# Softmax weights of a one-query attention laid out with four rows of one head side by side

## The chip, the core and the metric

The kernel runs on one core of a Trainium2 chip. The metric is device time in microseconds, the median of the runs of one kernel. Before the change it was 1253.28 us (three runs, 1253.01 to 1253.91). A profile shows the span of one execution on the device, some 2 us less than the time of the run.

## The reference

Eight batches of 32 heads, one query row per head, 4096 keys and values of 128 numbers each, all bfloat16:

```python
q: (8, 32, 1, 128)   k, v: (8, 32, 4096, 128)
scores = jnp.einsum('bhqd,bhkd->bhqk', q, k) * scale     # scale = 128 ** -0.5
attn = softmax(scores, axis=-1)
return jnp.einsum('bhqk,bhkd->bhqd', attn, v)
```

Every key and value is used once, for one multiply and one add, so there is little arithmetic per byte.

## The kernel before

The 256 heads are taken in 32 tiles of G = 8 heads. A tile of keys, kt, has 128 partitions, 16 for each head, and C = 256 rows per partition: 8 MB. VectorE (DVE) multiplies kt with the query and folds it in halves; TensorE (PE) adds up parts of it with an identity matrix; DVE reduces the result to scores, sc, 256 per partition. ScalarE (ACT) then makes the weights w. A value matmul here takes all 128 partitions of w and vt (128 x 32 and 128 x 512 in the profile of before) and sums over them, so w has a column for each of the eight heads at each row, and a bias of -1e30 makes those of foreign heads zero.

```python
sc_pool = ctx.enter_context(tc.tile_pool(name="sc_pool", bufs=1))
...
w = w_pool.tile([P, C, G], BF16, name="w", tag="w")
...
for g in range(G):
    nc.scalar.activation(
        out=w[:, :, g], in_=sc[:], func=ACT.Exp, bias=bias[:, g : g + 1], scale=scale,
        accum_out=esum[:, t % R, g : g + 1],
    )
```

A value matmul takes CB = 4 rows of w, 32 columns, as stationary operand and four rows of vt, 512 columns, as moving one. Its 32 x 512 result goes to one of four groups of PSUM partitions, av; the records of matmuls of different groups overlap (64 of them took 5.42 us in a middle tile, at a mean of 525 ns each). Only the blocks where the row of w equals the row of vt are wanted; a second matmul with a matrix of ones and zeros, pick, takes them out.

```python
group = [
    0 if t == NT - 1 and C // 2 <= c0 < C // 2 + 3 * C // 16 else c0 // CB % TG
    for c0 in range(0, end, CB)
]
for c0 in range(lo, hi, CB):
    i = c0 // CB
    j = group[i]
    nc.tensor.matmul(
        avs[t][j * AG : (j + 1) * AG, :], lhsT=w[:, c0 : c0 + CB, :],
        rhs=vt[:, c0 : c0 + CB, :], start=(i < TG), stop=(j not in group[i + 1 :]),
    )
...
for m in range(CB):      # result_of: pick the blocks out of the copy of av
    nc.tensor.matmul(
        ops[n][:], lhsT=pick[:, m, r, :], rhs=comb[:, m, :],
        start=(r == 0 and m == 0), stop=(r == R - 1 and m == CB - 1),
    )
```

In the last tile twelve successive matmuls go to one group, one after another. The last tile of vt comes in seven pieces of 128, 64, 32, 16, 8, 4 and 4 rows, so that its matmuls can follow the landings.

Of the kernel before, what the change touches and what calls it, by code (L numbers as in the profile page):

```python
# [7 lines left out]
ACT = mybir.ActivationFunctionType  # L8
ALU = mybir.AluOpType
AX = mybir.AxisListType  # L10
BF16 = mybir.dt.bfloat16
F32 = mybir.dt.float32

G = 8
KB, VB = 2, 1
TG = 4
R = 2
OB = 4
LAST = 4
# [4 lines left out]
def kernel(  # L24
# [7 lines left out]
    nc = tc.nc  # L32
    B, H, Sq, D = q.shape
    S = k.shape[2]
    P = nc.NUM_PARTITIONS
    assert Sq == 1 and D == 128
    NH = B * H
    PH = P // G
    C = S // PH
    NT = NH // G  # L40
    scale = float(D) ** -0.5
# [4 lines left out]
    CB = 4  # L46
    RG = R * G
    NQ = NT // R
    TB = 32
    AG = CB * G  # L50
    assert TG * AG == P and NH % P == 0 and P % G == 0 and TB % PH == 0 and C % CB == 0

    q_n = q.rearrange("b h o d -> (b h o) d").rearrange("(x p) d -> p x d", p=P)
    o_n = out.rearrange("b h o d -> (b h o) d").rearrange("(n u x) d -> n x u d", u=OB, x=RG)
# [7 lines left out]
    w_pool = ctx.enter_context(tc.tile_pool(name="w_pool", bufs=2))  # L62
# [14 lines left out]
        out=ident[:], in_=ident[:], pattern=[[-1, P]], compare_op=ALU.not_equal,  # L77
        fill=1.0, base=0, channel_multiplier=1,
# [5 lines left out]
        out=heads[:], in_=heads[:], pattern=[[-1, G], [0, PH]], compare_op=ALU.not_equal,  # L84
        fill=1.0, base=0, channel_multiplier=1,
# [5 lines left out]
        out=own[:], in_=own[:], pattern=[[-PH, G]], compare_op=ALU.is_ge,  # L91
        fill=NEG, base=0, channel_multiplier=1,
    )
    nc.gpsimd.affine_select(
        out=own[:], in_=own[:], pattern=[[PH, G]], compare_op=ALU.is_ge,
        fill=NEG, base=PH - 1, channel_multiplier=-1,
# [4 lines left out]
        out=same[:].rearrange("p (h x) -> p h x", x=PH),  # L101
        in_=own[:].rearrange("p (b h) -> p h b", h=TB // PH)
# [7 lines left out]
    for j in range(TG):  # L110
        part = pick[j * AG : (j + 1) * AG, :, :, :]
        nc.gpsimd.affine_select(
            out=part, in_=part, pattern=[[-G, CB], [G, R], [-1, RG]],
            compare_op=ALU.not_equal, fill=1.0, base=0, channel_multiplier=1,
        )
        nc.gpsimd.affine_select(
            out=part, in_=part, pattern=[[-G, CB], [0, R], [0, RG]],
            compare_op=ALU.is_ge, fill=0.0, base=0, channel_multiplier=1,
        )
        nc.gpsimd.affine_select(  # L120
            out=part, in_=part, pattern=[[G, CB], [0, R], [0, RG]],
            compare_op=ALU.is_ge, fill=0.0, base=G - 1, channel_multiplier=-1,
        )
    ones = consts.tile([P, 1], F32, name="ones")
    nc.vector.memset(ones[:], 1.0)
# [1 line left out]
    w_last = consts.tile([P, LAST, RG], BF16, name="w_last")  # L127
# [90 lines left out]
    def weights_of(t):  # L218
        sc = scs.pop(t)
        pmax = small.tile([P, 1], F32, name="pmax", tag="pmax")  # L220
        nc.vector.tensor_reduce(out=pmax[:], in_=sc[:], axis=AX.X, op=ALU.max)  # L221
        spread = small.tile([P, TB], F32, name="spread", tag="spread")
        nc.vector.tensor_scalar(  # L223
            out=spread[:], in0=same[:], scalar1=pmax[:, 0:1], scalar2=-scale,
            op0=ALU.add, op1=ALU.mult,
        )
        nmax = small.tile([P, 1], F32, name="nmax", tag="nmax")
        nc.vector.tensor_reduce(  # L228
            out=nmax[:], in_=spread[:], axis=AX.X, op=ALU.min, apply_transpose=True
        )  # L230
        bias = small.tile([P, G], F32, name="bias", tag="bias")
        nc.vector.tensor_scalar(  # L232
            out=bias[:], in0=own[:], scalar1=nmax[:, 0:1], scalar2=None, op0=ALU.add
        )
        w = w_pool.tile([P, C, G], BF16, name="w", tag="w")
        if t % R == 0:
            esums[t // R] = small.tile([P, R, G], F32, name="esum", tag="esum")
        esum = esums[t // R]
        for g in range(G):
            nc.scalar.activation(  # L240
                out=w[:, :, g], in_=sc[:], func=ACT.Exp, bias=bias[:, g : g + 1], scale=scale,
                accum_out=esum[:, t % R, g : g + 1],
            )
        ws[t] = w
        if t == NT - 1:
            nc.gpsimd.tensor_copy(out=w_last[:, :, RG - G : RG], in_=w[:, C - LAST : C, :])

    avs = {}

    def values_of(t, lo, hi):  # L250
        vt = loads["v", t]
        w = ws[t]
        if lo == 0:
            avs[t] = ps_v.tile([P, CB * D], F32, name="av", tag="av")
        end = C if t < NT - 1 else C - LAST
# [7 lines that stand above are left out]
            i = c0 // CB  # L263
            j = group[i]
            nc.tensor.matmul(  # L265
                avs[t][j * AG : (j + 1) * AG, :], lhsT=w[:, c0 : c0 + CB, :],
                rhs=vt[:, c0 : c0 + CB, :], start=(i < TG), stop=(j not in group[i + 1 :]),
            )

# [56 lines left out]
    with tc.manual_schedule():  # L326
        q_prep(0)
        for t in range(NT):
# [15 lines left out]
            if t > 0 and not v_last:  # L344
                values_of(t - 1, 0, C)
                copy_of(t - 1)
# [6 lines left out]
            if t > 0 and v_last:  # L353
                values_of(t - 1, 0, C)
            scores_of(t, 3)
            weights_of(t)
            if t > 0:
                if v_last:
                    copy_of(t - 1)
                if t % R == 0:  # L360
                    norm_of(n)
                result_of(t - 1)
        values_of(NT - 1, 0, C // 2)
        norm_of(NQ - 1)
        recip_of(NQ - 1)
# [34 lines left out]
```

## Time and profile before

| | before |
|---|---|
| time, us | 1253.28 |
| read from DRAM | 536.94 MB, at 429 GB/s over the span |
| busy share: DMA queue of k and v / DVE / PE / ACT | 99.4% / 83% / 40% / 27% |
| one exponential (ACTIVATE), ns | 1591 |
| read of its accumulator, ns | 496 |

The page of a profile gives busy shares in 40 slices, the chain of work that ended last, and groups of instructions with busy time and mean duration. The prediction shows these lines. One more group line belongs to them, that of the read of the sum that each exponential keeps (columns: line, engine, operation, names, shapes, count, then busy us, mean ns, idle time before):

```profile
L240 ACT ACTIVATION_READ_ACCUMULATOR w<-sc,bias 128x1 f32 x256 | 127.0, 496 | 0.0
```

There is one such read for each of the 256 exponentials, and its 496 ns overlap with the exponential that follows. Exponentials overlap too, so that 1591 ns is the time of one from start to end and not the time from one to the next. In the last group of the kernel before the starts lie some 1.1 us apart (start, duration, what):

```profile
1236.25 1.60 ACT L240 ACTIVATE w<-sc,bias 128x256 bf16<-128x256 f32 x1
1237.39 1.60 ACT L240 ACTIVATE w<-sc,bias 128x256 bf16<-128x256 f32 x1
```

### The profile page before, as it was taken

Reading aid. Unit: us, or ns where it says so; the run is one execution under the profiler, and the core shown is the slowest. Engines: PE = TensorE matmul, PEld = TensorE weight load, DVE = VectorE, ACT = ScalarE, POOL = GpSimd, SP = SyncE. Lnnn points to the kernel's source line nnn. Section 1 sums busy time; section 2 is a strip of 40 time slices with the busy share of each in tenths; the row PEclk is TensorE's granted clock in tenths of the full one; section 3 lists DMA queues with packets and bytes.
Section 4 is the critical chain, followed back from the end, with each engine's and each line's share of the span. In section 5 each row is a group of like instructions: output and inputs, shape, how many; then the busy total and the mean of one; then the engine's idle time right before and its main releaser. Section 6 shows DMA issues by size and latency. Waiting matters only on the chain.

```text
span 1251.5 us, 7723 instructions
## 1 busy us (share of the span) xinstructions
PE 501.8 (40%) x3067; PEld 176.1 (14%) x3067; DVE 1038.0 (83%) x588; ACT 343.8 (27%) x625; POOL 6.0 (0%) x26
## 2 busy tenths in 40 slices
PE   1334442444333443334533244432444334444455
PEld 0111110111111111111111111111111111111122
DVE  5888898888988889788898888987879888899981
ACT  0321233321333312333123331233321333213333
POOL 1000000000000000000000000000000000000000
PEclk9766655666556666566665666656666566666777
DMA  9999999999999999999999999999999999999997
GB/s 404 436 434 432 436 434 434 434 436 428 426 435 434 436 426 436 429 434 436 434 430 434 432 434 432 428 434 434 436 434 434 434 434 436 434 419 428 428 444 325
DMA packets 11444, 537.50 MB, mean 429 GB/s; under 512 B 1808, under 2 KB 2064, under 8 KB 2320
## 3 DMA queue, kind: packets, MB, share of 16 engines
q1 hardware_dynamic: 11072, 536.94, 99.4%
q8 instruction: 24, 0.39, 0.1%
q10 hardware_dynamic: 336, 0.07, 0.0%
q14 instruction: 12, 0.10, 0.0%
HBM read 536.94 MB, written 0.07 MB: 429 GB/s over the span
## 4 chain that ended last, share of the span: by engine, by line
DMA 76%; PE 15%; DVE 8%; issue 1%; SPq 0%; ACT 0%
DMA vt<-in_v_dram 75%; PE av L265 13%; DVE kt L179 5%; DVE kt L182 2%; PE ps L199 1%; DMA q_all<-in_q_dram 1%; DVE kt L187 0%; DVE sc L211 0%; SPq L146 0%; DVE pmax L221 0%; DVE spread L223 0%; DVE nmax L228 0%; ACT comb L292 0%; PE op L307 0%; ACT stage L316 0%
## 5 line engine op out<-in xcount | busy, mean ns | idle before, releaser
L179 DVE TENSOR_TENSOR kt<-kt,qb 128x8192 bf16<-128x8192 bf16 x128 | 565.1, 4415 | 91.3 <-DMA kt<-in_k_dram 79.8
L199 PE MATMUL ps<-kt,ident 128*128 128x512 bf16 x792 | 293.1, 529 | 662.8 <-DVE kt L187 507.4
L240 ACT ACTIVATE w<-sc,bias 128x256 bf16<-128x256 f32 x256 | 301.1, 1591 | 360.9 <-DVE bias L232 360.9
L182 DVE TENSOR_TENSOR kt<-kt 128x4096 bf16<-128x4096 bf16 x128 | 293.3, 2292 | 4.4
L199 PEld LDWEIGHTS <-ident 128*128 128x128 bf16 x792 | 92.0, 119 | 824.7 <-issue 670.0
L265 PE MATMUL av<-vt,w 128*32 128x512 bf16 x2047 | 181.0, 525 | 43.7 <-DMA vt<-in_v_dram 43.7
L211 DVE TENSOR_REDUCE sc<-ps 128x64 f32<-128x512 f32 x128 | 87.7, 685 | 87.0 <-PE ps L199 87.0
L292 ACT ACTIVATE comb<-av 128x512 bf16<-128x512 f32 x32 | 19.7, 616 | 413.2 <-PE av L265 413.2
L240 ACT ACTIVATION_READ_ACCUMULATOR w<-sc,bias 128x1 f32 x256 | 127.0, 496 | 0.0
L265 PEld LDWEIGHTS <-w 128*32 128x32 bf16 x2047 | 68.1, 127 | 167.7 <-issue 80.9
L187 DVE TENSOR_TENSOR kt<-kt 128x2048 bf16<-128x2048 bf16 x58 | 71.0, 1225 | 2.0
L162 ACT ACTIVATE qg<-qh 8x128 bf16<-8x128 f32 x32 | 8.5, 266 | 95.3 <-PE qh L158 95.3
L307 PE MATMUL op<-comb,pick 128*16 128x128 bf16 x128 | 16.4, 271 | 14.6 <-ACT comb L292 14.6
L221 DVE TENSOR_REDUCE pmax<-sc 128x1 f32<-128x256 f32 x32 | 13.4, 420 | 1.1
L285 DVE RECIPROCAL rz<-zp 16x1 f32<-16x1 f32 x16 | 2.4, 149 | 14.0 <-PE zp L277 14.0
L158 PE MATMUL qh<-q_all,ident 128*8 128x128 bf16 x32 | 8.5, 266 | 13.2 <-DMA q_all<-in_q_dram 13.2
L164 PE MATMUL qp<-qg,heads 8*128 8x128 bf16 x32 | 8.3, 258 | 12.7 <-ACT qg L162 12.7
L307 PEld LDWEIGHTS <-pick 128*16 128x16 bf16 x128 | 9.2, 104 | 26.2 <-issue 26.1
L316 ACT ACTIVATE stage<-op,rz 16x128 bf16<-16x128 f32 x16 | 6.2, 385 | 24.2 <-DVE rz L285 17.8
L166 ACT ACTIVATE qb<-qp 128x128 bf16<-128x128 f32 x32 | 8.9, 277 | 11.1 <-PE qp L164 11.1
L223 DVE TENSOR_SCALAR spread<-same,pmax 128x32 f32<-128x32 f32 x32 | 7.7, 241 | 1.1
L232 DVE TENSOR_SCALAR bias<-own,nmax 128x8 f32<-128x8 f32 x32 | 7.4, 231 | 1.1
(27 smaller groups left out, 26.8 us busy)
## 6 DMA issues: line engine op xcount, KB each, us to landing
kt<-in_k_dram SPq DMA_DIRECT2D x7, 4096.0 KB, 34.4
kt<-in_k_dram SPq DMA_DIRECT2D x2, 2048.0 KB, 36.7
vt<-in_v_dram SPq DMA_DIRECT2D x1, 4096.0 KB, 39.5
vt<-in_v_dram SPq DMA_DIRECT2D x1, 2048.0 KB, 44.0
vt<-in_v_dram SPq DMA_DIRECT2D x1, 1024.0 KB, 46.0
vt<-in_v_dram SPq DMA_DIRECT2D x1, 512.0 KB, 46.8
vt<-in_v_dram SPq DMA_DIRECT2D x31, 33.1
kt<-in_k_dram SPq DMA_DIRECT2D x28, 43.5
```

The lines of the kernel that those rows point to most:

```text
L158: nc.tensor.matmul(qh[:], lhsT=ident[:, p0 : p0 + G], rhs=q_all[:, x, :], start=True, stop=True)
L166: nc.scalar.activation(out=qb[:, 0, :], in_=qp[:], func=ACT.Copy)
L179: nc.vector.tensor_tensor(out=part, in0=part, in1=qb[:].to_broadcast([P, MC, D]), op=ALU.mult)
L182: nc.vector.tensor_tensor(out=part[:, :, 0 : D // 2], in0=part[:, :, 0 : D // 2], in1=part[:, :, D // 2 : D], op=ALU.add,)
L187: nc.vector.tensor_tensor(out=part[:, :, 0 : D // 4], in0=part[:, :, 0 : D // 4], in1=part[:, :, D // 4 : D // 2], op=ALU.add,)
L199: nc.tensor.matmul(ps[:], lhsT=ident[:], rhs=kt[:, u * UC : (u + 1) * UC, s * DS : (s + 1) * DS], start=(s == 0), stop=(s == n - 1),)
L211: nc.vector.tensor_reduce(out=scs[t][:, u * UC : (u + 1) * UC], in_=sums.pop((t, u))[:], axis=AX.X, op=ALU.add)
L221: nc.vector.tensor_reduce(out=pmax[:], in_=sc[:], axis=AX.X, op=ALU.max)
L240: nc.scalar.activation(out=w[:, :, g], in_=sc[:], func=ACT.Exp, bias=bias[:, g : g + 1], scale=scale, accum_out=esum[:, t % R, g : g + 1],)
L265: nc.tensor.matmul(avs[t][j * AG : (j + 1) * AG, :], lhsT=w[:, c0 : c0 + CB, :], rhs=vt[:, c0 : c0 + CB, :], start=(i < TG), stop=(j not i ...
L292: nc.scalar.activation(out=comb[:], in_=av, func=ACT.Copy)
L307: nc.tensor.matmul(ops[n][:], lhsT=pick[:, m, r, :], rhs=comb[:, m, :], start=(r == 0 and m == 0), stop=(r == R - 1 and m == CB - 1),)
```

## The change

One exponential writes a single head's weights. Before, these lie 16 bytes apart, with the seven other heads between them. The change puts four successive rows of one head side by side, 8 bytes, and steps 64 bytes from one such run to the next. The 32 columns of a value matmul are still 32 neighbouring numbers, now ordered by head and then by row, so pick gets another pattern (and needs two selects per group fewer) and the copy into w_last another order.

```diff
         nc.gpsimd.affine_select(
-            out=part, in_=part, pattern=[[-G, CB], [G, R], [-1, RG]],
+            out=part, in_=part, pattern=[[-1, CB], [CB * G, R], [-CB, RG]],
             compare_op=ALU.not_equal, fill=1.0, base=0, channel_multiplier=1,
         )
-        (two more affine_selects, which cleared what lay outside a row's heads)
...
-        w = w_pool.tile([P, C, G], BF16, name="w", tag="w")
+        w = w_pool.tile([P, C // CB, G, CB], BF16, name="w", tag="w")
...
+        sc_g = sc[:].rearrange("p (i m) -> p i m", m=CB)
         for g in range(G):
             nc.scalar.activation(
-                out=w[:, :, g], in_=sc[:], func=ACT.Exp, bias=bias[:, g : g + 1], scale=scale,
+                out=w[:, :, g, :], in_=sc_g, func=ACT.Exp, bias=bias[:, g : g + 1], scale=scale,
...
-            nc.gpsimd.tensor_copy(out=w_last[:, :, RG - G : RG], in_=w[:, C - LAST : C, :])
+            nc.gpsimd.tensor_copy(
+                out=w_last[:, :, RG - G : RG].rearrange("p m g -> p g m"),
+                in_=w[:, (C - LAST) // CB, :, :],
+            )
...
-                avs[t][j * AG : (j + 1) * AG, :], lhsT=w[:, c0 : c0 + CB, :],
+                avs[t][j * AG : (j + 1) * AG, :], lhsT=w[:, i, :, :],
```

More of the change, by code (lines that the diff above doesn't have):

```diff
@@ L50 @@
     AG = CB * G
-    assert TG * AG == P and NH % P == 0 and P % G == 0 and TB % PH == 0 and C % CB == 0
+    assert LAST == CB and TG * AG == P and NH % P == 0 and P % G == 0 and TB % PH == 0 and C % CB == 0
     q_n = q.rearrange("b h o d -> (b h o) d").rearrange("(x p) d -> p x d", p=P)
@@ L112 @@
         nc.gpsimd.affine_select(
-            out=part, in_=part, pattern=[[-G, CB], [G, R], [-1, RG]],
+            out=part, in_=part, pattern=[[-1, CB], [CB * G, R], [-CB, RG]],
             compare_op=ALU.not_equal, fill=1.0, base=0, channel_multiplier=1,
-        )
-        nc.gpsimd.affine_select(
-            out=part, in_=part, pattern=[[-G, CB], [0, R], [0, RG]],
-            compare_op=ALU.is_ge, fill=0.0, base=0, channel_multiplier=1,
-        )
-        nc.gpsimd.affine_select(
-            out=part, in_=part, pattern=[[G, CB], [0, R], [0, RG]],
-            compare_op=ALU.is_ge, fill=0.0, base=G - 1, channel_multiplier=-1,
         )
```

## The prediction

> **What bounds the kernel now.** I read the page's slices first, since they say whether any one resource is full from beginning to end.
>
> ```profile
> PE   1334442444333443334533244432444334444455
> ...
> DVE  5888898888988889788898888987879888899981
> ACT  0321233321333312333123331233321333213333
> ...
> DMA  9999999999999999999999999999999999999997
> GB/s 404 436 434 432 436 434 434 434 436 428 426 435 434 436 426 436 429 434 436 434 430 434 432 434 432 428 434 434 436 434 434 434 434 436 434 419 428 428 444 325
> ```
>
> Each digit is a tenth of busy time in one of 40 slices of 31.3 us. The row to look at is DMA: nine tenths or more in every slice but the last, and the rate row stands at 426 to 436 GB/s nearly throughout. DVE is high but not full, ACT mostly at two or three tenths. The DMA section of the page says how much has to come in.
>
> ```profile
> q1 hardware_dynamic: 11072, 536.94, 99.4%
> ...
> HBM read 536.94 MB, written 0.07 MB: 429 GB/s over the span
> ```
>
> Keys and values are read once, 536.94 MB. At the best common slice rate, 436 GB/s, that alone is 536.94 / 0.436 = 1231.5 us of the 1251.5 us span. So no change that leaves the bytes alone can take off more than 20.0 us (1.6%), and that bound also includes start and drain.
>
> Next the costly groups, for the lines that the change touches.
>
> ```profile
> L240 ACT ACTIVATE w<-sc,bias 128x256 bf16<-128x256 f32 x256 | 301.1, 1591 | 360.9 <-DVE bias L232 360.9
> L265 PE MATMUL av<-vt,w 128*32 128x512 bf16 x2047 | 181.0, 525 | 43.7 <-DMA vt<-in_v_dram 43.7
> L265 PEld LDWEIGHTS <-w 128*32 128x32 bf16 x2047 | 68.1, 127 | 167.7 <-issue 80.9
> ```
>
> After the bar stand busy us and mean ns of one, then the idle time before and what ended it. The exponentials take 1591 ns for 256 elements per partition; they wait for the maximum (bias), and the matmuls that use their result wait for vt from DRAM. No group shows PE waiting for the exponentials: w is ready before vt. The timeline of a middle tile agrees: the eight exponentials run from 623.5 to 632.9 us and the value matmuls that use them start at 645.65, when their vt lands. The slack is 12.8 us.
>
> Last the chain of waits at the end of the kernel, the one place where slack can vanish.
>
> ```profile
> 1200.13 46.92 DMA vt<-in_v_dram
> 1247.06 0.04 issue
> 1247.10 0.74 PE av L265 x3
> 1247.84 0.02 issue
> 1247.86 0.60 ACT comb L292
> 1248.47 0.04 issue
> 1248.51 0.40 PE op L307 x4
> 1248.91 0.02 issue
> 1248.93 0.36 ACT stage L316
> ```
>
> Columns are start, duration and what. The last pieces of vt land at 1247.06; three matmuls, a copy, four pick matmuls and a scaled copy follow, then the output's own DMA. The exponentials are not in it, but only just, as the timeline of PE shows:
>
> ```profile
> 1239.85 3.56 PE L265 MATMUL av<-vt,w 128*32 128x512 bf16 x29
> 1243.25 0.19 PE L277 MATMUL zp<-ones,esum 128*16 128x1 f32 x2
> 1243.30 3.61 PE L265 MATMUL av<-vt,w 128*32 128x512 bf16 x28
> 1247.10 0.72 PE L265 MATMUL av<-vt,w 128*32 128x512 bf16 x3 [0.19 <-DMA vt<-in_v_dram]
> ```
>
> The last tile's matmuls could not start before its exponentials ended (about 1239). They catch up at 1246.91 and still wait 0.19 us for the last vt. Two limits nearly meet there; DMA is the later one.
>
> [...]the copy of 512 elements takes 616 ns and that of 128 elements 277 ns (qb, line 166), so (616 - 277) / 384 = 0.88 ns per element, though both read PSUM.
> [...]in the two ten-microsecond windows filled with exponentials (623 to 633 and 662 to 672) DMA moved 439 and 446 GB/s; in the windows just after them 426 and 420. Slow writes do not cost DMA anything that could come back.
> [...]
>
> **The change part by part.**
> Exponentials. The count stays 256, the read of sc stays contiguous. [...] Issue spacing matters more for the group of eight: in the tail the starts are 1229.56, 1230.53, 1231.70 ... 1237.39, about 1.12 us apart, and the group ends near 1239.0, 9.4 us. [...] None of this is on the chain in the 31 tiles with slack of 12.8 us or so.
>
> Value matmuls. Still 2047 of them, with stationary columns that are 32 consecutive bf16 before and after; only their order differs. Loads stay at 127 ns, matmuls at 525 ns: 0. The pick matmuls likewise: 128 of 271 ns, another pattern of ones: 0.
>
> Prologue. Eight of twelve selects on POOL go, 8 x 0.34 = 2.7 us of POOL's 6.0 us. They end at about 7.1 us; pick is first used at 84.3 us. On the path: 0. The copy into w_last writes in another order, still 32 elements per partition; it took 0.21 us at 1239.1 and its user ran at 1247.77. Even at 1 us it stays hidden: 0.
>
> Tail. [...]the first half of vt lands near 1198.2 + 39.5 = 1237.7, taking the median to landing of the 4096 KB piece. So the first 32 matmuls start 1.8 us earlier, and then follow the pieces; the 0.19 us wait becomes longer, but the last landing, 1247.06, does not move. Its three matmuls and all that follow stay. Gain 0. A small loss is possible: PE now works in bursts, and its granted clock was 0.50 from 1239 to 1243 and 1.00 from 1244 on; should it be 0.50 at the end, three plus four plus four short matmuls, 0.72 + 0.38 + 0.38 us, might grow by 0.2 to 0.5 us.
>
> Sum: 1253.28 + 0 to 0.4, minus at most a few tenths for jitter in the order of DMA. I say 1253.3 us.
>
> **Rivals.**
> *Buffers come free earlier.* A faster ACT could free something that starts a load sooner. For: ACT also does the copy of av and q. Against: the copy in a middle tile (613.05) comes right after the matmuls, which ended by vt, and the issue of the next vt (612.99) preceded it; that queue already had the k tile in flight until 626.3, 13 us of supply. If wrong somewhere, the slices of 419 to 430 GB/s could rise to 434: some eight slices by 1 to 2%, 3 to 4 us, so 1249 to 1250.
> *The tail is bound by ACT rather than DMA.* For: only 0.19 us separates the two, and the DMA share drops to 0.54 to 0.68 from 1243 to 1247, so pieces may be there before the profile says. If all but the final four rows had landed early, the backlog of matmuls would vanish and the end could come up to 1 us sooner: 1252.3.
> *The new form is slower.* Each write of four is 8 bytes in a 64-byte step, and the output pattern has one dimension more. If it hurt, an exponential of 2500 ns would make the group 16 us: middle tiles still hide it under 12.8 us of slack plus nine already counted, but the tail would end 6 to 7 us later, about 1260. [...]
>
> **Range and chances.** Runs before spread over 0.9 us. The first rival gives the low side, the clock at the end and a different chip the high side: 1250.0 to 1255.5 us. Faster by over 2% needs 1228.2 us, below the 1231.5 us of pure transfer: 0.01. Slower by over 2% needs 1278.3, an exponential group some 34 us long: 0.01. Within 2%: 0.98.
>
> **What would show the steps right or wrong.** [...]the read of the accumulator, 496 ns, should stay. Loads and matmuls of av keep 127 and 525 ns within a few per cent; POOL has 18 instructions. DMA stays at 99% and 429 GB/s, the chain's end is again vt landing some 4.5 us before the span's end, with a longer wait ahead of the last av matmuls. A time below 1250 would say that ACT was releasing loads after all; one above 1256 that the new write or the clock of PE reached the tail.

The sum came to 1253.28 + 0 to 0.4 us, and the forecast to 1253.3 us. That the first 32 matmuls wait for the landing near 1237.7, and no longer for the exponentials, the profile after bears out (exponentials done at 1231.7, matmuls from 1237.35 on).

## The result

The kernel after took 1253.59 us (median of four runs, 1253.39 to 1253.93), the kernel before 1253.14 us in the same comparison. The ratio is 1.0003 with a 95% interval from 0.9985 to 1.002: the same. A ratio here is the mean time of one kernel's fast runs over that of the other's of the same rounds, so not quite the ratio of the medians.

The slices of the profile after, for ACT and DMA:

```profile
ACT  0111011111011110111101111011110111101111
...
DMA  9999999999999999999999999999999999999997
GB/s 404 436 434 434 436 434 436 432 436 432 434 437 430 431 432 432 436 432 434 432 432 432 436 436 434 434 425 430 433 430 434 432 432 436 432 430 431 427 448 308
```

ACT's digits fell from two or three to one; the DMA row did not change at all. Then the groups of the same kernel that answer to those of before:

```profile
L261 PE MATMUL av<-vt,w 128*32 128x512 bf16 x2047 | 183.5, 529 | 52.0 <-DMA vt<-in_v_dram 52.0
L233 ACT ACTIVATE w<-sc,bias 128x256 bf16<-128x256 f32 x256 | 126.3, 494 | 357.8 <-DVE bias L224 357.8
L261 PEld LDWEIGHTS <-w 128*32 128x32 bf16 x2047 | 67.8, 127 | 178.9 <-issue 86.8
L233 ACT ACTIVATION_READ_ACCUMULATOR w<-sc,bias 128x1 f32 x256 | 47.7, 186 | 0.0
```

An exponential fell from 1591 to 494 ns, and the read of its accumulator from 496 to 186 ns. From one start to the next it is now 0.49 us instead of some 1.1 us, so a group of eight takes 3.9 us instead of 9.4 us:

```profile
1228.23 0.49 ACT L233 ACTIVATE w<-sc,bias 128x256 bf16<-128x256 f32 x1
1228.72 0.49 ACT L233 ACTIVATE w<-sc,bias 128x256 bf16<-128x256 f32 x1
```

ACT's busy time was halved, from 343.8 to 172.6 us. The matmuls and loads of PE kept their durations. So 171 us of work went, and the time did not move. The end of the chain of waits of the kernel after (start, duration, what) differs from that of before:

```profile
1197.03 45.19 DMA vt<-in_v_dram
1242.22 0.04 issue
1242.26 6.08 PE av L261 x26
1248.34 0.02 issue
1248.36 0.61 ACT comb L288
```

Before, the chain came from the last landing of vt, at 1247.06, and the copy of av (comb) started at 1247.86. Here it comes from an earlier piece, landed at 1242.22, and 6.08 us of PE work; the copy starts 0.5 us later than before, although the loads were done no later (the DMA share is 0.00 from 1247 on). The experiments look into that, too.

### The profile page after: what moved, and what is told of

It is laid out like the page before. It is cut to its first block, busy times and chain, and to the rows that moved or that the text cites. A ratio compares the mean times of both kernels' runs of the same rounds, so it can differ in the third digit from the quotient of the medians.

```text
span 1252.0 us, 7714 instructions
## 1 busy us (share of the span) xinstructions
PE 503.5 (40%) x3067; PEld 175.8 (14%) x3067; DVE 1038.0 (83%) x588; ACT 172.6 (14%) x625; POOL 3.3 (0%) x18
## 4 chain that ended last, share of the span: by engine, by line
DMA 75%; PE 15%; DVE 8%; issue 1%; ACT 0%; SPq 0%
DMA vt<-in_v_dram 74%; PE av L261 14%; DVE kt L171 5%; DVE kt L174 2%; PE ps L191 1%; DMA q_all<-in_q_dram 1%; DVE kt L179 0%; DVE sc L203 0%; DVE pmax L213 0%; SPq L138 0%; DVE spread L215 0%; DVE nmax L220 0%; ACT comb L288 0%; PE op L303 0%; ACT stage L312 0%
## 5 line engine op out<-in xcount | busy, mean ns | idle before, releaser
L233 ACT ACTIVATE w<-sc,bias 128x256 bf16<-128x256 f32 x256 | 126.3, 494 | 357.8 <-DVE bias L224 357.8
L233 ACT ACTIVATION_READ_ACCUMULATOR w<-sc,bias 128x1 f32 x256 | 47.7, 186 | 0.0
L156 PE MATMUL qp<-qg,heads 8*128 8x128 bf16 x32 | 8.3, 259 | 12.7 <-ACT qg L154 12.7
```

Source lines behind the costliest of these rows:

```text
L233: nc.scalar.activation(out=w[:, :, g, :], in_=sc_g, func=ACT.Exp, bias=bias[:, g : g + 1], scale=scale, accum_out=esum[:, t % R, g : g + 1],)
```

## The experiments

All kernels passed the check of the result, except the two that load V only once, which are wrong. Twelve were run.

### What made an exponential slow

My theory was that a write is dear when none of the writes around it in time goes to a place near by. Three kernels change the order or place of the writes (and, to match, of what reads them) and nothing else. Each was run and profiled once. The first puts two rows side by side: 4 bytes, then a step of 32.

```diff
-        w = w_pool.tile([P, C // CB, G, CB], BF16, name="w", tag="w")
+        w = w_pool.tile([P, C // 2, G, 2], BF16, name="w", tag="w")
+        (sc_g, w_last, lhsT and pick to match)
```

> The kernel after with two rows of one head side by side instead of four: an exponential writes runs of 4 bytes with a step of 32 bytes[...]. Theory[...]: 494 ns as in the kernel after, ACT busy about 173 us. Rival (each jump costs something, and 64 jumps just hid under the other work): halfway, 650 to 1050 ns. Time unchanged by either, 1253 to 1254 us.

The second lets two heads alternate: four values of a head lie 4 bytes apart, so that no two of them are neighbours, and the next four begin 64 bytes on from these.

```diff
-        w = w_pool.tile([P, C // CB, G, CB], BF16, name="w", tag="w")
+        w = w_pool.tile([P, C // CB, G // 2, CB, 2], BF16, name="w", tag="w")
...
-                out=w[:, :, g, :], in_=sc_g, ...
+                out=w[:, :, g // 2, :, g % 2], in_=sc_g, ...
+        (w_last, lhsT and pick to match)
```

> The kernel after with the rows of two heads interleaved: an exponential writes single values 4 bytes apart[...], then jumps 32 or 64 bytes; no two of its writes are contiguous[...]. Theory[...]: 494 ns. Rival (contiguous runs count, each lone 2-byte write is dear): near 1600 ns as before, as there are 256 lone writes again. Time unchanged by either, 1253 to 1254 us.

The third fills the very places that the kernel after fills, but goes through all of them four times and each time writes one value of each run of four, 64 bytes from the one before.

```diff
-        sc_g = sc[:].rearrange("p (i m) -> p i m", m=CB)
+        sc_g = sc[:].rearrange("p (m i) -> p m i", m=CB)
...
-                out=w[:, :, g, :], in_=sc_g, ...
+                out=w[:, :, g, :].rearrange("p i m -> p m i"), in_=sc_g, ...
```

> The kernel after with the same places of w written by each exponential, but in another order: one value of each four, 64 bytes apart, then the second of each four, and so on; the scores are read in order as ever, so the weights are permuted and the result is wrong on purpose. [...] Time unchanged by either.

The two durations expected are near 1600 ns if it counts that successive writes are near each other, near 494 ns if only the places written count.

The result of this one was to be wrong, but the check passed it. The inputs q and k are normal numbers times 0.05, so the scaled scores spread by some 0.0025 (an estimate, 0.05 x 0.05) and all weights of a head are nearly equal. The check therefore doesn't tell a right order of weights from a wrong one; that the kernel after has them in the right places rests on reading its code.

The group of the exponentials in the profiles of the three, in this order, one fence for each; in the third, the read of the accumulator as well:

```profile
L235 ACT ACTIVATE w<-sc,bias 128x256 bf16<-128x256 f32 x256 | 127.4, 513 | 361.9 <-DVE bias L226 361.9
```

```profile
L235 ACT ACTIVATE w<-sc,bias 128x256 bf16<-128x256 f32 x256 | 134.0, 563 | 365.1 <-DVE bias L226 365.1
```

```profile
L233 ACT ACTIVATE w<-sc,bias 128x256 bf16<-128x256 f32 x256 | 298.3, 1582 | 356.1 <-DVE bias L224 356.1
L233 ACT ACTIVATION_READ_ACCUMULATOR w<-sc,bias 128x1 f32 x256 | 127.9, 500 | 0.0
```

Two values side by side suffice, but for 19 ns (513 against 494). Lone values 4 bytes apart cost 69 ns more than neighbours (563 against 494), no more, so runs without a gap are not what matters; where the 69 ns come from stays open. The third kernel fills the same places as the kernel after and takes 1582 ns, about as long as before, so not the places matter but the order. Writes whose neighbour in time lies 2 or 4 bytes away were fast (494, 513 and 563 ns), those 16 or 64 bytes from the next slow (1591 and 1582 ns); 8 bytes were not tried, and how nearness comes to count is not shown. The bytes written are the same in all three. The times, one run each, were 1253.05, 1253.98 and 1254.12 us, beside 1252.99 us of the kernel before for the first two and a median of 1253.22 us for the third: an exponential of 1582 ns or of 494 ns makes no difference to speak of.

### How much room there was

If loads bound the kernel, more exponentials should be free up to some limit. Both kernels were run with each group of eight done twice.

```diff
-        for g in range(G):
+        for g in list(range(G)) * 2:
             nc.scalar.activation(
```

> The kernel before with each group of eight exponentials run twice (same result). Theory (loads bound the kernel, the exponentials are hidden in every tile but the last, and in the last they just about meet the last landing): the group grows from 9.4 to some 18.8 us, still shorter than the 22 us between the first exponential of a middle tile (623.5) and the matmuls that use it (645.65), so middle tiles cost nothing; in the last tile the exponentials end 9.4 us later, 1248.4 instead of 1239.0, and the 12.5 us that follow them before the end follow again: about 1262 us, 9 us more. Rival A (hidden in the tail too, with room): within 1 us of 1253.3. Rival B (ACT releases loads in every tile): 32 times some microseconds, 1350 us or more.

> The kernel after with each group of eight exponentials run twice (same result). The group grows from 3.9 to 7.8 us; in the last tile it ends at 1235.5 instead of 1231.6, still ahead of the landing of the first half of the last vt at 1237.35. Theory: within 1 us of the kernel after (1253.6). Rival B (ACT releases loads): a good deal longer, 1270 us or more. Together with the other run this tells what the room is that the change made: 9.4 more us of exponentials cost 9 us before, 3.9 more cost nothing after.

The kernel after so doubled took 1254.6 us, ratio to before 1.0013 (0.9998 to 1.0028), as expected: 1.0 us from the 1253.59 us of the kernel after. But all four of its runs lie above all seven of the kernel before in the same rounds, by 1.6 us at the medians (1254.60 and 1252.99), and in its profile the last wait for vt ends at 1248.39, not at 1247.10 as in the kernel before; why is not shown. The kernel before so doubled took 1287.52 us, ratio 1.0272 (1.0257 to 1.0288), not 1262. Neither the theory nor a rival had that number. What DVE waited for in that run (total us, times, longest us):

```profile
DVE sc L211 <- PE ps L199: 103.4, 33, 9.9
DVE sc L211 <- ACT w L240: 87.8, 30, 5.3
```

The second line is new, and it stands in place of the 79.8 us for which DVE waits for loads of kt in the kernel before. The first reduction of the next tile's scores writes into sc, of which there is one buffer, and must wait until the last exponential has read the old scores. I had measured the room up to the reader of w: 12.8 us. The line that I had not looked at is in the timeline of DVE of the kernel before:

```profile
642.19 0.68 DVE L211 TENSOR_REDUCE sc<-ps 128x64 f32<-128x512 f32 x1
```

The exponentials ended at 632.9, so the room up to there was 9.3 us, and the doubled group needs 9.4 more. To test that, sc got two buffers. It takes 1 KB more per partition, and the store of results was made smaller along with it; a run with OB = 2 alone was not made.

```diff
-OB = 4
+OB = 2
...
-    sc_pool = ctx.enter_context(tc.tile_pool(name="sc_pool", bufs=1))
+    sc_pool = ctx.enter_context(tc.tile_pool(name="sc_pool", bufs=2))
+    (and the exponentials twice, as above)
```

> The kernel before with the exponentials run twice, and with two buffers for the scores (sc) instead of one; to make room the output stage holds 2 groups instead of 4, which makes the output's small stores more frequent. The run with doubled exponentials alone took 1287.5 us, not the 1262 expected; in its chain DVE's first sum of the next tile waits for the exponentials, which hold the only sc. Theory (that buffer is the nearest limit of a middle tile, 642.2 - 632.9 = 9.3 us of room in the kernel before, and not w with 12.8 us): with two buffers the wait of DVE for ACT goes, middle tiles are bound by loads again, and only the last two tiles pay, 9.4 us for the copy of av that PE waits for behind the exponentials of the last but one and 9.4 us for the last: about 1272 us. Rival (the order of ACT's own queue, where the query of the next tile stands behind the exponentials, is what holds the tiles up): 1284 us or more.

It took 1274.08 us, ratio 1.0164 (1.0147 to 1.0181), near the 1272 expected. In its list of waits DVE no longer waits for ACT because of sc. The rival's queue can be seen, PE waits 181.1 us in 32 times for the query behind the exponentials (12.7 us in the kernel before), but the time stays well under its 1284. What is left of the excess lies mostly in the last two tiles, in PE's timeline of this run:

```profile
1217.64 0.59 PE L307 MATMUL op<-comb,pick 128*16 128x128 bf16 x4 [16.78 <-ACT comb L292]
...
1261.00 0.37 PE L307 MATMUL op<-comb,pick 128*16 128x128 bf16 x2 [16.26 <-ACT comb L292]
```

PE stands idle for 16.78 and 16.26 us because the copy of av is queued on ACT behind a group of exponentials. In the kernel before the same two waits are 7.27 and 7.01 us, so they grew by 9.5 and 9.3 us. The 1262 expected of the first doubled run counted only one of the two. Ahead of the product DVE's waits are put down to ACT ten times in this run, 29.9 us, and to loads of kt 16 times, 52.9 us. Together that is 82.8 us in 26 waits, where the kernel before has 79.8 us in 25 for loads of kt; so the ten are probably waits for loads too, named wrongly by the profile. The last 2 us of the excess stay open.

### What the change is worth when loads are out of the way

V was loaded for the first tile only and used for all. The results are wrong.

```diff
     def load(kind, t):
+        if kind == "v" and t > 0:
+            loads["v", t] = loads["v", 0]
+            return
```

> The kernel before with V loaded for the first tile only and used for all (wrong result on purpose); half of the bytes go. Theory: loads need some 620 us then, and DVE's 1038 us of work become the bound: start 14.5 us, 1038 us, tail of exponentials 9.4 us, matmuls of the last tile 7.5 us and 5 us of drain, 1070 to 1090 us, with DVE over 94% busy. Rival B (ACT is on the path of every tile once loads are out of the way): DVE well under 94% busy and a time above 1120 us.

> The kernel after with V loaded for the first tile only (wrong result on purpose). Theory: DVE is the bound in every tile, ACT stays hidden, and the change is worth only what it takes off the last tile, where no load covers the exponentials: 9.4 - 3.9 = 5.5 us less than the kernel before with the same cut, so about 0.5% faster. Rival B: if ACT were on the path in each tile, up to 5.5 us a tile, 170 us less. Rival C (hidden in the tail too): no difference.

Before took 1178.43 us so, after 1171.72 us. Ratios to the unaltered kernel before are 0.9404 and 0.9347; one over the other gives 1.0061, 0.6% for the change, against the 0.5% expected. In the profiles both kernels had finished the last bias at the same time (1154.1 and 1154.3 us), and the last copy of results starts at 1172.60 and 1167.52: the whole difference comes after the last bias, in the one tile where no other work covers the exponentials. The lines are the last copy of results in before and in after, and then what DVE waited for in before:

```profile
1172.60 0.36 ACT L319 ACTIVATE stage<-op,rz 16x128 bf16<-16x128 f32 x1 [0.47 <-PE op L310]
1167.52 0.36 ACT L315 ACTIVATE stage<-op,rz 16x128 bf16<-16x128 f32 x1 [0.47 <-PE op L306]
...
DVE sc L214 <- PE ps L202: 94.1, 33, 3.1
```

The absolute times were some 90 to 110 us longer than I expected, and DVE was 88% busy and not 94%. By the signs that I had set (well under 94%, above 1120 us) that would be rival B for the kernel before. It is refuted all the same: the change gained 6.7 us and not 170, exponentials are 1.6% of the chain of before, and DVE's list of waits does not name them. My theory had left out a wait that the trace of before shows too: DVE stands idle some 3 us a tile until PE has added up the last part of the scores, 94 us in total here (87 in the kernel before).

### The end of the last tile

Four kernels were run together over five rounds: the kernel after once more; both kernels without the twelve matmuls in one group; and the kernel after without these and with matmuls that nobody reads, so that PE is not idle while pieces of vt land.

> The kernel after, unaltered, once more beside the kernel before and the variants of this call, over five rounds. Both theories: ratio within 0.2% of 1; in the profile the last value matmuls end about 1 us after the last load has landed, where before they ended 0.5 us after it.

```diff
-            0 if t == NT - 1 and C // 2 <= c0 < C // 2 + 3 * C // 16 else c0 // CB % TG
+            c0 // CB % TG
```

> The kernel after without the special grouping in the last tile that sends twelve successive value matmuls to one column group. Theory (in the kernel after, the twelve matmuls start cold, at a granted clock of 0.50 and some 0.43 us each[...]; 5.1 us in a row put the end of the value matmuls behind the last landing): without it [...]those of a piece end before the next piece lands, and the value matmuls end some 0.5 to 0.9 us sooner, right after the last landing, with a last wait on DMA of vt; time 0.4 to 0.9 us less than the kernel after. Rival (the last landing alone sets the end): value matmuls end where they ended, within 0.2 us relative to the last landing.

> The kernel before without that special grouping. There the value matmuls of the last tile ran from 1239.5 on without a gap and with the clock up to 1.00 from 1243; the twelve in one group cost 0.2 us each and were done at the last landing. Theory: without them PE runs dry, waits for the last landing longer, may end at a lower clock; the end moves by less than 0.5 us either way. Rival (the special grouping costs the same before and after): 0.4 to 0.9 us less here as well.

```diff
+        keep_warm(14)                       # 14 matmuls ident x kt into an unused ps
         values_of(NT - 1, 0, C // 2)
+        keep_warm(12)
         norm_of(NQ - 1)
```

> The kernel after without the special grouping, and with matmuls that nobody reads between the value matmuls of the last two tiles (14) and between the two halves of the last (12), so that PE doesn't stand idle while vt lands. Theory (the loss in the tail is the low clock): the granted clock is 1.00 from about 1236 on, value matmuls end within 0.3 us of the last landing, and the end comes about 1 us sooner than in the kernel after and 0.3 to 0.5 us sooner than in the kernel before. If the special grouping alone was the cause, this run ends as the one without it, within 0.2 us.

| kernel | time, us | ratio to before (95%) | copy of av starts (profile), us |
|---|---|---|---|
| before | 1253.02 | | 1247.86 |
| after, first run | 1253.59 (other rounds) | 1.0003 (0.9985 to 1.002) | 1248.36 |
| after, once more | 1253.20 | 1.0002 (0.9990 to 1.0015) | 1247.65 |
| after, no single group | 1253.44 | 1.0002 (0.9988 to 1.0015) | 1247.78 |
| before, no single group | 1253.00 | 0.9999 (0.9987 to 1.0012) | 1247.80 |
| after, PE kept busy | 1253.20 | 1.0001 (0.9988 to 1.0013) | 1247.54 |

No time differs. (The copy of before is from its first profile.) Without the single group the kernel before ended within 0.1 us of before, as expected. The profiles of the others do tell something, at a scale of 0.8 us. The unaltered kernel after ended its value matmuls 0.7 us sooner in its second profile than in its first. The difference is the clock that PE was granted, shown here in windows of three microseconds (window, its length, busy us and counts of PE, PEld, DVE, ACT and POOL, clock, DMA share, GB/s), first profile and second profile:

```profile
1240.00:1243.00 3.00, 1.72 (x16) 0.63 (x9) 0.15 (x1) 0.00 (x0) 0.00 (x0) 0.50 0.88 355
1243.00:1246.00 3.00, 3.00 (x8) 1.05 (x7) 0.00 (x0) 0.00 (x0) 0.00 (x0) 0.50 0.62 246
```

```profile
1240.00:1243.00 3.00, 1.53 (x17) 0.70 (x10) 0.15 (x1) 0.00 (x0) 0.00 (x0) 0.89 0.88 355
1243.00:1246.00 3.00, 2.89 (x23) 1.27 (x22) 0.00 (x0) 0.00 (x0) 0.00 (x0) 1.00 0.63 252
```

At 0.50 only eight matmuls, from among the twelve that go one after another, fit into the three microseconds from 1243 on, at 1.00 twenty-three. In the first profile PE is then the last to finish; in the second the chain ends again with the landing of vt. The two single runs with two rows side by side and with mixed heads, which keep the short exponentials and the twelve matmuls, show both again: clock 0.97 from 1240 to 1243 and the copy at 1247.49, clock 0.50 and the copy at 1248.54. So the same kernel can have either clock there, and the time of the tail varies by some 0.8 us with it; what decides in a run is not shown. Taking the twelve matmuls out brought the end of the value matmuls to 1247.78, 0.6 us sooner than the slow profile, but no sooner than the fast one; with PE kept busy the clock was 1.00 from 1237 to 1246 (without, 0.50, 0.82 and 0.75 in the three windows), but 0.50 from 1248 on, where the four pick matmuls took 0.58 and not 0.38 us. My expectation of about 1 us less than the kernel after was too high: it compared with the one slow profile.

## Why the prediction was right

The time, 1253.59 us, lies within the range, 0.3 us from the predicted 1253.3. The main reason holds: the bytes set the time. Removing 171 us of ACT's busy time left the DMA row as it was, and with half of the bytes gone the change gave what the last tile gives and no more. By its steps:

- **The exponential.** Measured were 494 ns instead of 1591, and 513 ns with two values side by side. The spacing was 0.49 us instead of some 1.12 (starts at 1227.72, 1228.23, 1228.72), the group ended near 1231.7 instead of 1239.0, and ACT's busy time fell from 343.8 to 172.6 us.
- **"The read of the accumulator, 496 ns, should stay."** This was wrong: 186 ns. It was 500 ns again in the third kernel, where each write lay 64 bytes from the one before, so it goes with the writes of the exponential before it; why is not shown.
- **Value and pick matmuls, prologue, w_last.** Predicted 0, and no cost is seen: 529 and 127 ns for the value matmuls and their loads, 265 instead of 271 ns for the picks, 18 instructions on POOL. The copy into w_last grew from 209 to 318 ns and stayed hidden.
- **The tail.** "The last landing does not move" and a possible loss of 0.2 to 0.5 us by PE's clock were both stated. The loss came in the first profile (the copy 0.5 us later than before) and not in the second (0.2 us sooner). It came in another place than stated: the short matmuls at the end ran at 1.00 and took 0.39 and 0.38 us; the twelve value matmuls that go one after another were the ones at 0.50. That the number fits is in part luck. (In the kernel after without the single group the short ones did take 0.58 us at 0.50.) The claim that the chain's end would again be vt landing with a longer wait ahead of the last matmuls held only in the second. In the windows the clock is 0.50, 1.00 or between (0.82, 0.89), and one kernel had 0.50 in one profile and 1.00 in the other from 1243 to 1246; what decides is not shown.
- **The rivals.** *Buffers come free earlier* is refuted for the change: no load gained. *The tail is bound by ACT* did not come true, as the time did not fall. *The new form is slower* did not either, but its reasoning has the one step that failed: "middle tiles still hide it under 12.8 us of slack plus nine already counted". The doubled run of before showed a nearer limit, the only sc buffer, 9.3 us away, and a second one, the copy of av behind the exponentials in ACT's queue, which PE waits for. With it fails "an exponential group some 34 us long" as what 2% slower needs: a group of 18.6 us already took 1287.5 us. The slack was enough for the change in either reckoning, so the predicted time didn't suffer.

Where did the gain of 171 us go? In all but the last two tiles it became idle time of ACT, since w, sc and the copy of av were ready in time before. In the last two it shortened a wait that the prediction's "no group shows PE waiting for the exponentials" had missed, as it stands under the name of the copy of av, queued behind them (before, then after):

```profile
L307 PE MATMUL op<-comb,pick 128*16 128x128 bf16 x128 | 16.4, 271 | 14.6 <-ACT comb L292 14.6
L303 PE MATMUL op<-comb,pick 128*16 128x128 bf16 x128 | 15.9, 265 | 4.6 <-ACT comb L288 4.6
```

In the first profile the last exponentials then started 1.8 us sooner (0.9 us in the second) and ended 7 us sooner, and PE waited for vt instead.

## What to carry to other kernels

When a chain of loads is full from the first slice to the last, a faster engine beside it may gain nothing, as here (171 us less of ACT's work, ratio 1.0003), however much its own busy time falls; first divide the bytes by the best slice rate and see what could be gained at all. Where ScalarE writes with a step, try to put at least two successive elements side by side, which took the exponential here from 1591 to 513 ns; other engines and types were not tried. When you measure the slack of a group of instructions, look for the first user of everything that it holds: what it writes, what it reads, and what stands behind it in its own queue.
